# Summing a gate by matmuls on four column groups, in the result's row order, instead of a pass through DRAM

## The chip, the core and the metric

The kernel runs on one core of one Trainium2 chip. The metric is device microseconds of one execution, lower is better; the time of a kernel is the median of several runs. One further execution is taken by the hardware profiler, and all rows below are from it.

## The reference

Two blocks read the same `x` (`A_q`, 2048 rows of 640) and a gate per row mixes them. Block A is a short causal convolution of `k`, a product with `v`, a long convolution along the sequence (done by FFT) and a product with `x`. Block B is local attention with 32 heads of 20, a window of 8 keys at a distance of 2, between two projections.

```python
x = A_q
g = sigmoid((x * gate_w).sum(-1, keepdims=True))      # one number per row of x
a = A(x, A_k, A_v, A_shift_k, A_ssm_k, A_ssm_D)       # x * (longconv(kv) + kv * D)
b = B(x, B_wqkv, B_wo)                                # attention(x @ wqkv) @ wo
out = g * a + (1 - g) * b
```

## The kernel before

The kernel is one long stream of small units of work. Each unit (a generator step) asks a planner, `Plan`, for an engine, with a cost, with what it depends on and with a priority, and `Plan.run` decides at build time in which order the units stand on each engine and which of four PSUM slots (`ps0` to `ps3`, two banks each) a TensorE tile takes. On the chip each engine then works off its row in that order. A unit that must wait holds up all that stands behind it on its engine, and a tile whose slot is still to be copied out waits for that very slot, even if another is free: the slot is fixed by the plan.

The stages, in order of time:

- `transposes` (L423) bring x into `xT`, with the row order of the attention: even rows, then odd rows. `vproj` (L439, tiles `psv`) and `qkproj` (L480, tiles `pj`, one per feature tile `ft` and per q or k) project. Copies to SBUF go to ScalarE or VectorE, whichever the planner picks (helper lines L237 and L239). `conv` (L400, VectorE, tiles `pa`, `pb`) makes `kv`; its last step of each quarter (L418) needs the loads of v.
- Attention, in eight passes of four heads: `score_gen` (L552, tiles `sc`, ten groups a pass, an Exp on ScalarE at L572 each) and `pv_gen` (L579, tiles `O`, two a pass of 32 and 36 matmuls, divided into `oS` by VectorE at L610 and L612).
- `h_stream` and `u_stream`: two transforms in two steps, s1 (L631, 8 matmuls a unit) and s2 (L649, 32 matmuls a unit), with a copy of 1024 columns after each unit: to `Am` after s1, to `Hs` (h) or `Up` (u) after s2. The filter's transform h has 20 units of s1 and 20 of s2.
- `otrans` (L799), products of the two transforms (L758, L761), `inverse1` (L775), `inverse2` (L848), and `outproj` (L883), whose copies scale by `omg` = 1 - g (L892). The results stand by `[partition 32*gg + p, tile t]` for row 64*p + 16*gg + t.

The gate (L457) is a stream with priority 6 that waits for the transposes and for the first half of `vproj`. It makes 80 matmuls with 128 columns of `xT` as weights and one moving column (`wg`), which leave the sums in `xT`'s order in `gps`. ScalarE takes the Exp of the whole (L466), VectorE makes the sigmoid (L468, L469) in `g_chk`. Two DMAs on GpSimd's queue write it to DRAM (L471, L472), four read it back in the result's order into `g_nat` (L475), and VectorE makes `omg` (L477). `g_nat` is read again at L826, `omg` at L892.

Of the kernel before, what the change touches and what calls it, by code (L numbers as in the profile page):

```python
# [11 lines left out]
F32 = mybir.dt.float32  # L12
ACT = mybir.ActivationFunctionType
ALU = mybir.AluOpType
PSUM = bass.MemoryType.PSUM
DRAM = bass.MemoryType.DRAM

S = 2048
D = 640
# [3 lines left out]
NDT = 5  # L23
# [4 lines left out]
PRE = 7  # L28
HS = 1024 + PRE
# [73 lines left out]
def ccol(sb):  # L103
    return PRE + 128 * sb + (PRE if sb >= 8 else 0)
# [105 lines left out]
def kernel(  # L210
# [14 lines left out]
    nc = tc.nc  # L225
# [6 lines left out]
    def raw(ap, off, dims):  # L232
        return bass.AP(tensor=ap.tensor, offset=ap.offset + off, ap=dims)
# [7 lines left out]
    p0 = ctx.enter_context(tc.tile_pool(name="p0", bufs=1))  # L241
    psp = ctx.enter_context(tc.tile_pool(name="psp", bufs=1, space=PSUM, reuse_waits="tile"))
    plan = Plan(4)

    def psum(g, name, shape=(128, 2, 512), dt=F32, k=0):
        t_ = psp.tile(list(shape), dt, name=name, tag=f"ps{g.banks[k]}")
        return t_
# [8 lines left out]
    G = Gs[:].rearrange("p (a r b) -> p a r b", a=32, r=2)  # L256
# [2 lines left out]
    M = p0.tile([128, 2, 128], BF, name="M")  # L259
    g_nat = p0.tile([128, 16], F32, name="g_nat")  # L260
    omg = p0.tile([128, 16], F32, name="omg")
    g_chk = p0.tile([128, 16], F32, name="g_chk")
    dpool = ctx.enter_context(tc.tile_pool(name="scratch_dram", bufs=1, space=DRAM))
    g_scr = dpool.tile([S], F32, name="g_scr")
    valid = p0.tile([128, NB], BF, name="valid")
    wg = p0.tile([128, NDT], BF, name="wg")
    sH = p0.tile([128, 2 * KW], BF, name="sH")
# [19 lines left out]
    xT = pL.tile([128, NDT, XW], BF, name="xT")  # L287
# [10 lines left out]
    def ev(name):  # L298
        if name not in E:
            E[name] = Ev()  # L300
        return E[name]

    def mark(name, g):
        x = ev(name)
        x.t, x.eng = g.done.t, g.done.eng
# [130 lines left out]
    def xdeps(c):  # L436
        return [ev(f"xT{c}{d}") for d in (0, 4)]

    def vproj():  # L439
        for half in range(2):  # L440
            c0 = 320 * half
            for b0 in range(0, NB, 2):
                nb = min(2, NB - b0)
                g = yield Req("P", 5 * nb * 136.0, xdeps(min(3, (b0 + nb - 1) // 4)) + [ev("Wv")], take=1, pri=2 if half == 0 else 4)
                ps = psum(g, "psv")
                for bb in range(nb):
                    for dt in range(NDT):
                        nc.tensor.matmul(ps[:, bb, 0:320], lhsT=xT[:, dt, BP * (b0 + bb):BP * (b0 + bb) + 128], rhs=Wv[:, dt, c0:c0 + 320],  # L448
                                         start=(dt == 0), stop=(dt == NDT - 1))
                if b0 == NB - 1:  # L450
                    mark(f"vproj{half}", g)
                r = yield Req("AD", n=320 * nb, deps=[g.done], give=g.banks, pri=-2)
                copy(r.eng, VW[:, b0:b0 + nb, 16 * half:16 * half + 16, 0:DH].rearrange("p b h d -> p b h d"),
                     ps[:, 0:nb, 0:320].rearrange("p b (h d) -> p b h d", h=16))
            mark(f"VW{half}", r)

    def gate():  # L457
        g = yield Req("P", 2200.0, xdeps(3) + [ev("vproj0")], take=1)
        gps = psum(g, "gps", (128, 16))
        for sb in range(16):  # L460
            for dt in range(NDT):
                nc.tensor.matmul(gps[:, sb:sb + 1], lhsT=xT[:, dt, ccol(sb):ccol(sb) + 128], rhs=wg[:, dt:dt + 1],
                                 start=(dt == 0), stop=(dt == NDT - 1))
        mark("gatePE", g)
        r = yield Req("A", 250.0, [g.done], give=g.banks)
        nc.scalar.activation(g_chk[:], gps[:], ACT.Exp, scale=-1.0)  # L466
        r = yield Req("D", 500.0, [r.done])
        nc.vector.tensor_scalar(g_chk[:], g_chk[:], 1.0, None, ALU.add)  # L468
        nc.vector.reciprocal(g_chk[:], g_chk[:])  # L469
        r = yield Req("G", 1000.0, [r.done], move=2000.0)  # L470
        nc.gpsimd.dma_start(g_scr[:].rearrange("(h s p two) -> p two h s", p=128, two=2, h=1)[:, 0, 0, :], g_chk[:, 0:8])  # L471
        nc.gpsimd.dma_start(g_scr[:].rearrange("(h s p two) -> p two h s", p=128, two=2, h=1)[:, 1, 0, :], g_chk[:, 8:16])  # L472
        r = yield Req("G", 4000.0, [r.done], move=500.0)
        for q in range(4):
            nc.gpsimd.dma_start(g_nat[32 * q:32 * q + 32, :], raw(g_scr[:], 16 * q, [[64, 32], [1, 16]]))  # L475
        r = yield Req("D", 150.0, [r.done])
        nc.vector.tensor_scalar(omg[:], g_nat[:], -1.0, 1.0, ALU.mult, ALU.add)  # L477
        mark("gate", r)

# [444 lines left out]
    plan.add(conv(), 6)  # L924
    plan.add(transposes(), 1)
    plan.add(vproj(), 2)
    plan.add(gate(), 6)
    plan.add(qkproj(), 3)
    plan.add(h_diag(), 0)
    plan.add(h_stream(), 5)  # L930
# [42 lines left out]
```

## Time and profile before

| | |
|---|---|
| median of 3 runs (lowest to highest) | 305.73 us (304.98 to 306.28) |
| the profiled execution: its time | 305.71 us |
| the profiled execution: span of the profile | 303.9 us |
| TensorE matmul busy | 231.3 us (76%) |
| ScalarE busy | 180.9 us (60%) |
| VectorE busy | 173.8 us (57%) |
| GpSimd busy | 78.5 us (26%) |
| mean granted TensorE clock | 0.851 of full speed |

No engine is busy throughout, so busy shares alone say little: the stages have different limits. The profile's chain that ended last says for each stage what was waited for, and the rows of single engines say what a wait holds up. PE is TensorE, DVE VectorE, ACT ScalarE, POOL GpSimd. A row of a timeline is a run of like instructions; a bracket at its end is the idle time of the engine ahead of it and who ended that.

### The profile page before, as it was taken

Reading aid. Unit: us, or ns where it says so; the run is one execution under the profiler, and the core shown is the slowest. Engines: PE = TensorE matmul, PEld = TensorE weight load, DVE = VectorE, ACT = ScalarE, POOL = GpSimd, SP = SyncE. Lnnn points to the kernel's source line nnn. Section 1 sums busy time; section 2 is a strip of 40 time slices with the busy share of each in tenths; the row PEclk is TensorE's granted clock in tenths of the full one; section 3 lists DMA queues with packets and bytes.
Section 4 is the critical chain, followed back from the end, with each engine's and each line's share of the span. In section 5 each row is a group of like instructions: output and inputs, shape, how many; then the busy total and the mean of one; then the engine's idle time right before and its main releaser. Section 6 shows DMA issues by size and latency. Waiting matters only on the chain.

```text
span 303.9 us, 10648 instructions
## 1 busy us (share of the span) xinstructions
PE 231.3 (76%) x4825; PEld 169.7 (56%) x4825; DVE 173.8 (57%) x220; ACT 180.9 (60%) x218; POOL 78.5 (26%) x147
## 2 busy tenths in 40 slices
PE   2893999935999999877787359998949792985820
PEld 2662565512555576755575258787838672963610
DVE  0226191048789789655557068965857587626610
ACT  1342354832588897987867436786656534877520
POOL 9879455304216225310002200000000020003320
PEclk9999899985999999755559659999978897899795
DMA  6999998987294124798007800000360998004530
GB/s 223 355 172 150 143 173 152 165 139 99 67 167 92 23 72 89 128 183 340 6 2 94 188 3 4 4 4 2 80 202 9 226 218 177 2 5 121 146 88 0
DMA packets 57789, 34.33 MB, mean 113 GB/s; under 512 B 49848, under 2 KB 54460, under 8 KB 56720
## 3 DMA queue, kind: packets, MB, share of 16 engines
q1 hardware_dynamic: 52432, 23.50, 38.1%
q0 software_dynamic: 5312, 10.16, 16.3%
q8 instruction: 37, 0.61, 0.9%
q14 instruction: 8, 0.07, 0.1%
HBM read 20.33 MB, written 2.63 MB: 76 GB/s over the span
## 4 chain that ended last, share of the span: by engine, by line
PE 41%; SPq 19%; DVE 15%; ACT 7%; issue 7%; DMA 6%; POOL 1%; POOLq 0%; DVEq 0%; ACTq 0%
SPq L315 19%; PE i L775 8%; PE pj L501 7%; PE op L883 5%; PE sc L565 5%; PE O L598 4%; PE psv L448 4%; DVE Hs L758 3%; DVE Hw L761 3%; DVE Am L239 3%; PE s L649 3%; DMA g_scr<-g_chk 3%; PE s L631 3%; ACT ET L572 2%; DMA g_nat<-g_scr 2%
## 5 line engine op out<-in xcount | busy, mean ns | idle before, releaser
L572 ACT ACTIVATE ET<-sc 128x726 bf16<-128x726 f32 (+1 forms) x80 | 65.1, 861 | 19.9 <-PE sc L565 19.3
L501 PE MATMUL pj<-xT,Wqk 128*128 128x363 bf16 (+3 forms) x250 | 52.3, 360 | 4.7 <-DVE VW L239 4.6
L239 DVE CAST Am<-s 128x1024 bf16<-128x1024 f32 x25 | 30.0, 1222 | 18.7 <-PE s L631 18.7
L649 PE MATMUL s<-Am,Gs 64*128 64x64 bf16 x1280 | 29.5, 200 | 13.5 <-DVE Hs L239 7.3
L565 PE MATMUL sc<-qb,kb 31*128 31x121 bf16 x544 | 28.1, 249 | 14.6 <-DVE oS L612 8.7
L501 PEld LDWEIGHTS <-Wqk 128*128 128x128 bf16 x250 | 23.7, 101 | 25.6 <-issue 7.9
L649 PEld LDWEIGHTS <-Gs 64*128 64x128 bf16 x1280 | 26.1, 102 | 17.6 <-issue 16.1
L565 PEld LDWEIGHTS <-kb 31*128 31x128 bf16 x544 | 15.5, 105 | 28.9 <-issue 18.2
L448 PE MATMUL psv<-Wv,xT 128*128 128x320 bf16 x170 | 27.0, 310 | 1.3 <-DVE xT L239 1.2
L775 PE MATMUL i<-M,Hw 128*128 128x128 bf16 x160 | 25.4, 250 | 2.9 <-issue 2.9
L883 PE MATMUL op<-wo,Hb 128*32 128x512 bf16 (+1 forms) x640 | 26.0, 310 | 1.1 <-ACT yg L857 0.7
L237 ACT CAST Cm<-i 128x1024 bf16<-128x1024 f32 x20 | 19.9, 1024 | 10.8 <-PE i L775 10.8
L775 PEld LDWEIGHTS <-Hw 128*128 128x128 bf16 x160 | 22.1, 154 | 3.8 <-issue 3.8
L775 PE MATMUL i<-M,Hs 128*128 128x128 bf16 x128 | 21.8, 258 | 0.7 <-ACT Am L237 0.4
L237 ACT CAST Gs<-pj 128x968 bf16<-128x968 f32 (+5 forms) x15 | 11.7, 782 | 17.2 <-PE pj L501 17.0
L237 ACT CAST Up<-s 128x1024 bf16<-128x1024 f32 x14 | 13.7, 1021 | 13.8 <-DVE Hw L761 13.8
L883 PEld LDWEIGHTS <-Hb 128*32 128x32 bf16 x640 | 18.2, 137 | 6.2 <-issue 2.2
L448 PEld LDWEIGHTS <-xT 128*128 128x128 bf16 x170 | 16.3, 101 | 8.9 <-POOL ET L373 1.2
L814 POOL DMA_DIRECT2D qg<-in_A_q_dram x4 | 1.9, 490 | 73.2 <-PE s L631 73.2
L537 POOL DMA_DIRECT2D qb<-Gs x21 | 10.6, 505 | 33.1 <-PE sc L565 28.3
L598 PEld LDWEIGHTS <-ET 128*128 128x128 bf16 x544 | 16.2, 100 | 4.6 <-issue 3.5
L775 PEld LDWEIGHTS <-Hs 128*128 128x128 bf16 x128 | 18.0, 154 | 1.1 <-issue 0.4
(81 smaller groups left out, 391.8 us busy)
## 6 DMA issues: line engine op xcount, KB each, us to landing
Hw<-Hs SPq DMA_DIRECT2D x8, 512.0 KB, 5.8
xS<-in_A_q_dram SPq DMA_DIRECT2D x4, 640.0 KB, 8.3
Hb<-in_A_k_dram SPq DMA_DIRECT2D x8, 320.0 KB, 12.5
kv<-in_A_v_dram SPq DMA_DIRECT2D x16, 160.0 KB, 7.2
Hb<-in_A_ssm_k_dram SPq DMA_DIRECT2D x16, 160.0 KB, 3.9
qg<-in_A_q_dram POOLq DMA_DIRECT2D x4, 640.0 KB, 8.0
Gs<-cf_G SPq DMA_DIRECT2D x1, 2048.0 KB, 11.2
Wqk<-in_B_wqkv_dram SPq DMA_DIRECT2D x2, 800.0 KB, 15.0
```

Source lines behind the costliest of these rows:

```text
L237: nc.scalar.copy(dst, src)
L239: nc.vector.tensor_copy(dst, src)
L315: nc.sync.dma_start(dst, src)
L448: nc.tensor.matmul(ps[:, bb, 0:320], lhsT=xT[:, dt, BP * (b0 + bb):BP * (b0 + bb) + 128], rhs=Wv[:, dt, c0:c0 + 320], start=(dt == 0), sto ...
L501: nc.tensor.matmul(ps[:, i, 0:n], lhsT=Wqk[:, dt, w, 128 * ft:128 * ft + 128], rhs=rhs, start=(dt == 0), stop=(dt == NDT - 1))
L537: nc.gpsimd.dma_start(dst[r0:r0 + fb - fa, 0:wd], stg[fa - f0:fb - f0, 0:wd])
L565: nc.tensor.matmul(sc[:, hh, BP * bb:BP * bb + BP], lhsT=kb[r:r + DH + NF, 128 * b:128 * b + 128], rhs=qb[r:r + DH + NF, BP * b:BP * b + B ...
L572: nc.scalar.activation(ETs[e][:, :, 0:nw], sc[:, :, 0:nw], ACT.Exp, scale=SCALE)
L598: nc.tensor.matmul(O[:, o0:o0 + 21], lhsT=ET[:, hh, BP * bb:BP * bb + 128], rhs=VW[:, b, 4 * t + h4, :], start=True, stop=True, skip_group ...
L649: nc.tensor.matmul(o, lhsT=G[rows, j, rr, :], rhs=Am[rows, 2 * j + rr, :, :], start=(rr == 0), stop=(rr == 1), tile_position=(64 * c, 0), ...
L775: nc.tensor.matmul(o, lhsT=src[:, c, :, :, 8 * oc + il].rearrange("p q j -> p (q j)"), rhs=M[:, k, :], start=(k == 0), stop=(k == 1), skip ...
L883: nc.tensor.matmul(op[32 * gg:32 * gg + 32, n0:n1], lhsT=raw(a, HS * (t % 2) + t // 2 + 8 * gg, [a.ap[0], [32, 32]]), rhs=wo[:, ft, n0:n1] ...
```

## The change

The gate is summed in the result's row order. For each of 16 result tiles t and each of 5 feature tiles, four matmuls stand side by side on the four column groups of TensorE, each with 32 columns of `xT` at a step of 32 as weights (rows 64*p + 16*gg + t) and the one moving column of `wg`: 320 matmuls instead of 80. The Exp goes straight to `g_nat`, VectorE makes the sigmoid in place and `omg` right after. The two DMAs out, the four back, `g_chk` and the DRAM scratch are gone. The stream no longer waits for `vproj`, its priority goes from 6 to 3, and its cost to the planner from 2200 to 5000.

```diff
     def gate():
-        g = yield Req("P", 2200.0, xdeps(3) + [ev("vproj0")], take=1)
+        g = yield Req("P", 5000.0, xdeps(3), take=1)
         gps = psum(g, "gps", (128, 16))
-        for sb in range(16):
+        for t in range(16):
             for dt in range(NDT):
-                nc.tensor.matmul(gps[:, sb:sb + 1], lhsT=xT[:, dt, ccol(sb):ccol(sb) + 128], rhs=wg[:, dt:dt + 1],
-                                 start=(dt == 0), stop=(dt == NDT - 1))
+                a = xT[:, dt, 0:1]
+                for gg in range(4):
+                    nc.tensor.matmul(gps[32 * gg:32 * gg + 32, t:t + 1],
+                                     lhsT=raw(a, PRE + HS * (t % 2) + t // 2 + 8 * gg, [a.ap[0], [32, 32]]), rhs=wg[:, dt:dt + 1],
+                                     start=(dt == 0), stop=(dt == NDT - 1), tile_position=(0, 32 * gg), skip_group_check=True)
         mark("gatePE", g)
         r = yield Req("A", 250.0, [g.done], give=g.banks)
-        nc.scalar.activation(g_chk[:], gps[:], ACT.Exp, scale=-1.0)
-        r = yield Req("D", 500.0, [r.done])
-        nc.vector.tensor_scalar(g_chk[:], g_chk[:], 1.0, None, ALU.add)
-        nc.vector.reciprocal(g_chk[:], g_chk[:])
-        r = yield Req("G", 1000.0, [r.done], move=2000.0)
-        nc.gpsimd.dma_start(g_scr[:]..., g_chk[:, 0:8])
-        nc.gpsimd.dma_start(g_scr[:]..., g_chk[:, 8:16])
-        r = yield Req("G", 4000.0, [r.done], move=500.0)
-        for q in range(4):
-            nc.gpsimd.dma_start(g_nat[32 * q:32 * q + 32, :], raw(g_scr[:], 16 * q, [[64, 32], [1, 16]]))
-        r = yield Req("D", 150.0, [r.done])
+        nc.scalar.activation(g_nat[:], gps[:], ACT.Exp, scale=-1.0)
+        r = yield Req("D", 650.0, [r.done])
+        nc.vector.tensor_scalar(g_nat[:], g_nat[:], 1.0, None, ALU.add)
+        nc.vector.reciprocal(g_nat[:], g_nat[:])
         nc.vector.tensor_scalar(omg[:], g_nat[:], -1.0, 1.0, ALU.mult, ALU.add)
         mark("gate", r)
...
-    plan.add(gate(), 6)
+    plan.add(gate(), 3)
```

With it the planner's whole order changes. Line numbers fall by 3 behind the removed declarations and by 7 behind the gate. The rows below give order only.

VectorE, before: the row around the first `kv` product (L418). `pa` and `pb` are the convolution, `rd` and `oS` the division behind the first `O` tile.

```order
L415 TENSOR_TENSOR pa<-pa,pb 128x2560
L418 TENSOR_TENSOR kv<-pa,kv 128x16x2x80
L407 TENSOR_TENSOR pa<-Hb,wl 128x2560
L407 TENSOR_TENSOR pb<-Hb,wl 128x2560
L415 TENSOR_TENSOR pa<-pa,pb 128x2560
L610 RECIPROCAL rd_81<-O 121x32
L612 TENSOR_TENSOR oS<-O,rd_81 121x8x80
L239 CAST Gs<-pj 128x768
```

VectorE at the same place, now:

```order
L412 TENSOR_TENSOR pa<-pa,pb 128x2560
L468 TENSOR_SCALAR g_nat<-g_nat 128x16
L469 RECIPROCAL g_nat<-g_nat 128x16
L470 TENSOR_SCALAR omg<-g_nat 128x16
L415 TENSOR_TENSOR kv<-pa,kv 128x16x2x80
L404 TENSOR_TENSOR pa<-Hb,wl 128x2560
L239 CAST sH<-pj 128x968
L404 TENSOR_TENSOR pb<-Hb,wl 128x2560
L603 RECIPROCAL rd_77<-O 121x32
L605 TENSOR_TENSOR oS<-O,rd_77 121x8x80
```

All of the gate now stands ahead of the `kv` product, and behind it VectorE copies out a projection (`sH`, ft = 2 of q) after one step of the convolution instead of dividing an `O` tile after three.

TensorE, before: the ninth of the ten groups of scores of the first pass, whose tile takes the slot of the first `O` tile (freed by L612 on VectorE). A bracket names whose semaphore is waited for.

```order
L501 LDWEIGHTS Wqk
L501 MATMUL pj<-xT,Wqk 128x384
L565 LDWEIGHTS kb_87 [waits DVE_49]
L565 MATMUL sc<-qb_88,kb_87 128x121 [waits PE_49]
L565 LDWEIGHTS kb_87
```

TensorE, now: the sixth group of the first pass, whose tile takes the slot of the projection that VectorE copies to `sH`.

```order
L494 LDWEIGHTS Wqk
L494 MATMUL pj<-xT,Wqk 128x363
L558 LDWEIGHTS kb_83
L558 MATMUL sc<-qb_84,kb_83 128x121 [waits DVE_49]
L558 LDWEIGHTS kb_83
```

The first instruction of TensorE that waits for VectorE's work behind the `kv` product is now three groups of scores earlier; the first `O` tile, two runs of 5 and 10 projections and 10 matmuls of `psv`, which stood ahead of it, stand behind it. The 320 matmuls of the gate stand ahead of ft = 1, where the 80 stood behind the last `psv`.

VectorE, before: the row behind the last division of the attention.

```order
L612 TENSOR_TENSOR oS<-O,rd_82 121x4x80
L468 TENSOR_SCALAR g_chk<-g_chk 128x16
L469 RECIPROCAL g_chk<-g_chk 128x16
L239 CAST Hs<-s_2472 128x8x128
L239 CAST Hs<-s_2518 128x8x128
L239 CAST Am<-s_2597 128x4x64x4
L239 CAST Am<-s_2641 128x4x64x4
L239 CAST Am<-s_2689 128x4x64x4
L477 TENSOR_SCALAR omg<-g_nat 128x16
L239 CAST Hs<-s_2745 128x8x128
```

VectorE at the same place, now:

```order
L605 TENSOR_TENSOR oS<-O,rd_78 121x4x80
L239 CAST Am<-s_2876 128x4x64x4
L239 CAST Am<-s_2920 128x4x64x4
L239 CAST Am<-s_2965 128x4x64x4
L239 CAST Am<-s_3009 128x4x64x4
L239 CAST Am<-s_3053 128x4x64x4
L239 CAST Am<-s_3097 128x4x64x4
L239 CAST Hs<-s_3152 128x8x128
```

`omg` no longer stands between the copies of the filter's transform. Between the last `psv` and the last `O`, TensorE now has 9 units of s1 and 5 of s2 where it had 6 and 1, 228 matmuls of scores where it had 248, and no gate; from the last `O` to the first `tr` it has 11 and 10 units where it had 14 and 14.

## Rows read from the trace of the kernel before

**Rows 1.** The chain that ended last, in order of time: start us, us, what.
```profile
160.05 8.14 DMA g_scr<-g_chk
...
170.46 5.92 DMA g_nat<-g_scr
```

**Rows 2.** By stretch: window, length, busy us of PE, PEld, DVE, ACT, POOL, clock, DMA.
```profile
71.99:120.65 48.66, 48.32 (x664) 28.58 (x666) 40.78 (x47) 37.38 (x48) 19.50 (x39) 0.95 0.43 85
120.65:157.77 37.12, 29.32 (x684) 22.07 (x686) 21.11 (x30) 31.29 (x41) 4.52 (x9) 0.56 0.54 135
...
166.62:176.51 9.89, 2.82 (x83) 2.19 (x81) 0.01 (x2) 3.76 (x4) 2.03 (x4) 0.63 0.68 157
```

**Rows 3.** Timeline of VectorE, filter's transform: start us, us, instructions, idle before.
```profile
159.67 2.29 DVE L239 CAST Hs<-s 128x1024 bf16<-128x1024 f32 x2
162.57 2.36 DVE L239 CAST Am<-s 128x1024 bf16<-128x1024 f32 x2 [0.62 <-PE s L631]
165.40 1.22 DVE L239 CAST Am<-s 128x1024 bf16<-128x1024 f32 x1 [0.47 <-PE s L631]
176.51 0.18 DVE L477 TENSOR_SCALAR omg<-g_nat 128x16 f32<-128x16 f32 x1 [9.88 <-DMA g_nat<-g_scr]
```

**Rows 4.** Timeline of TensorE, same stretch and its two ends.
```profile
155.23 1.03 PE L649 MATMUL s<-Am,Gs 64*128 64x64 bf16 x32
156.08 0.62 PE L631 MATMUL s<-F1b,Hb 64*128 64x128 bf16 x8
...
177.86 1.04 PE L649 MATMUL s<-Am,Gs 64*128 64x64 bf16 x32 [7.33 <-DVE Hs L239]
...
184.07 2.56 PE L799 MATMUL tr<-ident,oS 121*128 121x121 bf16 x45 [0.18 <-ACT Hs L237]
```

**Rows 5.** Timeline of ScalarE, same stretch.
```profile
159.68 2.85 ACT L237 CAST Am<-s 128x1024 bf16<-128x1024 f32 x3
162.40 3.06 ACT L237 CAST Hs<-s 128x1024 bf16<-128x1024 f32 x3
```

**Rows 6.** Timeline of VectorE, around the first kv product.
```profile
64.86 1.49 DVE L418 TENSOR_TENSOR kv<-pa,kv 128x2560 bf16<-128x2560 bf16 x1 [17.79 <-DMA kv<-in_A_v_dram]
66.38 1.49 DVE L407 TENSOR_TENSOR pa<-Hb,wl 128x2560 bf16<-128x2560 bf16 x1
```

**Rows 7.** Timeline of TensorE, ahead of that product and after it.
```profile
41.24 12.00 PE L501 MATMUL pj<-xT,Wqk 128*128 128x484 bf16 x65
...
71.99 0.48 PE L565 MATMUL sc<-qb,kb 31*128 31x121 bf16 x6 [8.58 <-DVE oS L612]
```

**Rows 8.** Timeline of TensorE at full clock: what one run of each kind takes.
```profile
91.23 0.95 PE L501 MATMUL pj<-xT,Wqk 128*128 128x363 bf16 x5
...
95.30 1.26 PE L501 MATMUL pj<-xT,Wqk 128*128 128x512 bf16 x5
...
98.31 1.53 PE L448 MATMUL psv<-Wv,xT 128*128 128x320 bf16 x10
99.78 0.34 PE L565 MATMUL sc<-qb,kb 31*128 31x121 bf16 x6
100.05 0.97 PE L598 MATMUL O<-VW,ET 128*128 128x21 bf16 x32
...
101.22 0.99 PE L501 MATMUL pj<-xT,Wqk 128*128 128x384 bf16 x5
```

**Rows 9.** The chain: the gate's matmuls, and matmuls on column and row groups.
```profile
120.97 2.08 PE gps L462 x80
...
194.20 1.51 PE op L883 x38
...
268.25 0.95 PE i L848 x96
```

**Rows 10.** Tile view of the gate: durations ns min/median/max, first and last start.
```profile
L462 PE MATMUL gps<-wg,xT x80: 163/163/178, 120.9 to 122.9; 128*128 128x1 bf16 x80
```

**Rows 11.** Line view of outproj: 640 weight loads of 32 columns at a step.
```profile
L883 PEld LDWEIGHTS <-Hb x640: 131/134/162, 194.1 to 290.0; 128*32 128x32 bf16 x160
```

More of the change, by code (lines that the diff above doesn't have):

```diff
@@ L261 @@
     omg = p0.tile([128, 16], F32, name="omg")
-    g_chk = p0.tile([128, 16], F32, name="g_chk")
-    dpool = ctx.enter_context(tc.tile_pool(name="scratch_dram", bufs=1, space=DRAM))
-    g_scr = dpool.tile([S], F32, name="g_scr")
     valid = p0.tile([128, NB], BF, name="valid")
@@ L457, in gate @@
     def gate():
-        g = yield Req("P", 2200.0, xdeps(3) + [ev("vproj0")], take=1)
+        g = yield Req("P", 5000.0, xdeps(3), take=1)
         gps = psum(g, "gps", (128, 16))
-        for sb in range(16):
+        for t in range(16):
             for dt in range(NDT):
-                nc.tensor.matmul(gps[:, sb:sb + 1], lhsT=xT[:, dt, ccol(sb):ccol(sb) + 128], rhs=wg[:, dt:dt + 1],
-                                 start=(dt == 0), stop=(dt == NDT - 1))
+                a = xT[:, dt, 0:1]
[3 more added lines that the diff above has]
+                                     start=(dt == 0), stop=(dt == NDT - 1), tile_position=(0, 32 * gg), skip_group_check=True)
         mark("gatePE", g)
         r = yield Req("A", 250.0, [g.done], give=g.banks)
-        nc.scalar.activation(g_chk[:], gps[:], ACT.Exp, scale=-1.0)
-        r = yield Req("D", 500.0, [r.done])
-        nc.vector.tensor_scalar(g_chk[:], g_chk[:], 1.0, None, ALU.add)
-        nc.vector.reciprocal(g_chk[:], g_chk[:])
-        r = yield Req("G", 1000.0, [r.done], move=2000.0)
-        nc.gpsimd.dma_start(g_scr[:].rearrange("(h s p two) -> p two h s", p=128, two=2, h=1)[:, 0, 0, :], g_chk[:, 0:8])
-        nc.gpsimd.dma_start(g_scr[:].rearrange("(h s p two) -> p two h s", p=128, two=2, h=1)[:, 1, 0, :], g_chk[:, 8:16])
-        r = yield Req("G", 4000.0, [r.done], move=500.0)
-        for q in range(4):
-            nc.gpsimd.dma_start(g_nat[32 * q:32 * q + 32, :], raw(g_scr[:], 16 * q, [[64, 32], [1, 16]]))
-        r = yield Req("D", 150.0, [r.done])
+        nc.scalar.activation(g_nat[:], gps[:], ACT.Exp, scale=-1.0)
+        r = yield Req("D", 650.0, [r.done])
+        nc.vector.tensor_scalar(g_nat[:], g_nat[:], 1.0, None, ALU.add)
+        nc.vector.reciprocal(g_nat[:], g_nat[:])
         nc.vector.tensor_scalar(omg[:], g_nat[:], -1.0, 1.0, ALU.mult, ALU.add)
```

## The prediction

> **What bounds the kernel now.** I read the chain that ended last first, since the busy shares of the four engines (26% to 76%) name no single limit. It shows the gate's way through DRAM on the path: 8.14 us until the write has landed and 5.92 us until the read has [rows 1]. Then I took the rows of the engines at that place to see what this wait holds up. On VectorE the small instruction that makes `omg` waits 9.88 us for the read, and the copies of the filter's transform stand behind it [rows 3]. TensorE runs out of PSUM slots and sits idle for 7.33 us, until VectorE copies again [rows 4]; in that stretch of 9.89 us VectorE is busy for 0.01 us, TensorE for 2.82 and ScalarE for 3.76 [rows 2]. The reader is to see that the wait is not the gate's own: `omg` is first used much later, and what costs is the place in VectorE's row.
>
> The busy times by stretch tell the limits elsewhere. From 71.99 us to the last `psv` at 120.65 us TensorE is busy for 48.32 of 48.66 us, so it sets the pace there. From there to the last `O` at 157.77 us nobody is full: ScalarE 31.29 and TensorE 29.32 of 37.12 us, at a mean granted clock of 0.56, so mostly at the lower level of 1.2 GHz [rows 2]. Ahead of 71.99 us VectorE waits 17.79 us for the loads of v with the first `kv` product [rows 6], and TensorE waits 8.58 us for what stands behind that product [rows 7].
>
> **The change, part by part.** All sums are made against the profiled execution, 305.71 us, which is within 0.02 us of the median of the three runs (305.73).
>
> *The wait goes, and with it part of the transform's work.* `omg` now depends on ScalarE and VectorE alone and is made before the first `kv` product, so nothing of the round trip is left. Between the last `O` (157.77) and the first `tr` (184.07 [rows 4]) lie 26.3 us for 28 units, 14 of s1 and 14 of s2. Where the copies run without the wait, from 159.67 to 166.62 us, VectorE makes five [rows 3] and ScalarE six [rows 5]: 11 units in 6.95 us, 0.63 us a unit. The new order leaves 21 units in this stretch, since seven more stand ahead of the last `O`. So 21 x 0.63 = 13.2 us, and 1.3 us as before until the copies run densely: 14.5 us, which is 11.8 us less. Of these, 7 x 0.63 = 4.4 us are moved units and 7.4 us the wait itself. TensorE's idle time of 7.33 us and VectorE's of 9.88 us bound the latter from both sides; I stay near the lower end because ScalarE made four copies during the wait (3.76 us [rows 2]), which now take their own time. What is late next there is the rate of the copies.
>
> *The matmuls of the gate.* Before, 80 take 2.08 us, 26 ns each, behind the last `psv` [rows 9]. 320 on four column groups have no row here. From below: 96 small matmuls on row and column groups take 0.95 us, 10 ns each [rows 9], so 3.2 us. From above, if every load and its matmul went one after the other: 134 ns for the load of 32 columns at a step [rows 11] and 163 ns for a matmul of one column [rows 10], 297 ns, so 95 us. The nearest row is `outproj`, with the same weights, on the same four groups: 38 pairs in 1.51 us, 40 ns each, with 128 or 512 moving columns [rows 9]; 12.7 us at most, and with one moving column surely less. I take 26 ns, the row of the old gate: 8.3 us. The Trainium skill, page "TensorE: Matmul & The Clock Gate", section "The mechanism", speaks against the change: a load of weights overlaps a running matmul only if their row groups differ, and here all 320 use all rows; by it the sum would be that of the third rival below. The `outproj` rows disagree, since 134 ns of load alone, 38 times in a row, would be 5.1 us and not 1.51.
>
> *Where these matmuls lie, and the new stall.* They stand ahead of ft = 1, so at 41.24 us. What comes before TensorE's next wait for VectorE: the 65 projections of the row at 41.24 (12.0 us [rows 7]), five more of 363 columns (0.95) and five groups of scores (0.34 each, 1.7 [rows 8]), in all 14.6 us. So TensorE arrives at the sixth group of scores at 55.9 us plus the gate's time. The slot it needs is that of the projection which VectorE now copies after `kv` and one step of the convolution: the loads end the wait at 64.86 us as before, since no load is touched, then 1.49 to 66.38, 1.49 to 67.9 [rows 6], and 1.16 us for 968 columns (1.22 for 1024 [rows 3]): 69.1 us. TensorE thus waits 13.2 us less the gate's time, and the gate costs nothing up to 13.2 us; at 8.3 us that cover holds. If the cover were gone, its whole time would be on the path, as TensorE is the bound behind it. The two gate instructions on VectorE ahead of `kv` and `omg`, some 0.6 us, and ScalarE's Exp lie within VectorE's 17.79 us of waiting; the queue behind them is the `kv` product itself, which could not have started earlier.
>
> TensorE starts again at 69.1 instead of 71.99 us, 2.9 us earlier, but with more to do. Behind the wait now stand 5 projections of 363 columns (0.95), 10 of 512 (2 x 1.26), 10 of 384 (2 x 0.99), 10 of `psv` (1.53), one `O` of 32 (0.97) and six groups of scores (6 x 0.34), all of which stood ahead of it before: 10.0 us by durations, some 9.5 us when the overlap of one run with the next (0.05 to 0.07 us) is taken off [rows 8]. Since TensorE is full until the last `psv`, this ends at 120.65 - 2.9 + 9.5 = 127.25 us: **6.6 us later**. This is the price of the new order, and nothing in the diff tells it.
>
> *From the last `psv` to the last `O`.* TensorE's 29.32 us lose the gate (2.08) and three groups of scores (about 0.5 each at the lower clock, between 0.34 and twice that, 1.5) and gain three units of s1 (0.62) and four of s2 (1.03 [rows 4]), 6.0: 31.7 us. ScalarE's 31.29 us over 41 instructions lose three Exps, about 2.3, and have 29.0 us. So from below 31.7 us. From above, if TensorE's idle time of 7.8 us stays, 39.5. Part of that idle time came from the gate, whose tile held one of four slots through this whole stretch because its Exp stood behind the last of the attention on ScalarE; now it is free at the start. I take 34.0 us, a good third of the idle time: 3.1 us less than before.
>
> *Removed, at nothing.* Six DMAs leave GpSimd's queue; what stands behind them there, the load of q, waits for the u transform long after, so nothing moves.
>
> **The sum.** +6.6 - 3.1 - 11.8 = -8.3 us; all later work keeps its order. 305.71 - 8.3 = **297.4 us**.
>
> **The rivals.**
>
> 1. *TensorE's lateness doesn't carry* (290.8 us). If the copies on VectorE (40.78 of 48.66 us) and ScalarE (37.38) set the pace in part, the 9.5 us of extra work would hide and the 6.6 us fall away: 297.4 - 6.6. Against it stands 48.32 of 48.66 us. Chance 0.20.
> 2. *The stretch to the last `O` doesn't get shorter* (302.9 us). If TensorE stays at the lower clock, with seven more units and the idle time it had, the stretch takes 39.5 us instead of 34.0: 297.4 + 5.5. A wait of s2 for its table, whose load follows the last `kv` product and so is some 6 us later too, would end in the same place. For it: the mean clock of 0.56. Against it: the free slot. Chance 0.20.
> 3. *Slower: the gate's pairs run one after the other* (about 379 us). Beyond the cover of 13.2 us every nanosecond counts: with p per pair, 320 p - 13.2 us is added, and the change loses from 320 p = 13.2 + 8.3, p = 67 ns. At 297 ns it is 95.0 - 13.2 = 81.8 us: 297.4 + 81.8 = 379. Against it: 40 ns per pair in `outproj`, with far longer matmuls. Chance 0.04.
>
> That the change doesn't do what it says can't be here: `omg` has no DMA left to wait for.
>
> **How the numbers follow.** Forecast 0.56, rivals 0.20, 0.20 and 0.04. The range takes in both middle rivals with a little beyond, 290 to 303.5 us. A measurement of this kernel can tell some 0.5% from no change, so 304.2 us is the limit: forecast, the first rival and most of the second lie below it, 0.93 faster. The tail of the second beyond 304.2 gives 0.03 for no change, and the third 0.04 for slower.
>
> **What would show it.** Right: the 320 matmuls start at about 41 us and end in under 13; TensorE then sits idle to about 69 us, its wait ended by VectorE's copy to `sH`; the last `psv` ends near 127 us, the last `O` near 161, the first `tr` near 176, with no idle time of VectorE over 2 us in between. Wrong: a last `psv` near 121 us would say that TensorE was not the bound; a stretch to the last `O` of over 38 us would say that the moved units were not free; an idle VectorE before `tr` would say that another wait took the place of `omg`'s. My least certain term is the 3.1 us.

## The result, and the profile after

The changed kernel takes **292.59 us** (median, 290.68 to 296.11), the kernel before beside it 305.63 us (304.98 to 306.28): a ratio of 0.955, 95% interval 0.946 to 0.964. Two later measurements gave 0.968 (0.965 to 0.971) and 0.959 (0.953 to 0.966). So it is faster by 3 to 5%, 13.0 us in the first measurement where 8.3 were forecast, and inside the range of 290 to 303.5 us. The profiled execution took 296.11 us (span 294.3), the slowest of the four and 3.5 us above the median; the rows below are from it and are compared with the sum, not with the median.

Cut at the points that the prediction names, in us:

| stretch | before | forecast | after | two further profiles of after |
|---|---|---|---|---|
| to the end of the last `psv` | 120.65 | 127.25 | 124.38 | 127.32, 128.79 |
| to the end of the last `O` | 37.1 | 34.0 | 34.4 | 33.3, 33.5 |
| to the first `tr` | 26.3 | 14.5 | 17.6 | 15.1, 16.6 |
| from there to the end | 119.9 | 119.9 | 118.0 | 117.3, 118.2 |

The two further profiles are of `e0_after` (294.73 us, beside a median of 294.27) and `e10_after` (298.81 us, the slowest of its six).

The page first: granted clock by slice, the queue of code, and the chain's shares by engine.

```profile
PEclk9998695799999999985555789999968897898675
...
q8 instruction: 39, 0.64, 1.0%
...
PE 54%; issue 12%; DVE 10%; ACT 7%; POOL 7%; DMA 5%; DVEq 0%; ACTq 0%; POOLq 0%
```

SyncE's queue, 19% of the chain before, is gone from it: the chain no longer runs through the loads of v. TensorE has 54% instead of 41, and "issue" 12% instead of 7. The long fall of the clock (slices 19 to 22) was there before; that of the seventh and eighth slice is new, while one that the kernel before had in its tenth slice is gone.

The gate and what follows, TensorE's timeline (start, us, engine, line, operation, tiles, count, idle time before):

```profile
42.47 2.11 PE L461 MATMUL gps<-wg,xT 128*32 128x1 bf16 x136
45.02 1.99 PE L461 MATMUL gps<-wg,xT 128*32 128x1 bf16 x128 [0.44 <-issue]
49.57 0.97 PE L461 MATMUL gps<-wg,xT 128*32 128x1 bf16 x56 [2.56 <-issue]
50.48 9.00 PE L494 MATMUL pj<-xT,Wqk 128*128 128x484 bf16 x35
...
67.56 0.34 PE L558 MATMUL sc<-qb,kb 31*128 31x121 bf16 x6
...
69.01 2.04 PE L494 MATMUL pj<-xT,Wqk 128*128 128x363 bf16 x10
```

The gate takes 8.07 us, of which it runs 5.07: 15.5 ns a pair of load and matmul (128 in 1.99 us). At 67.56 stands the sixth group of scores, where TensorE waited 8.58 us before [rows 7] and was to wait until 69.1 now. It does not wait at all. VectorE's timeline shows why:

```profile
50.81 0.17 DVE L468 TENSOR_SCALAR g_nat<-g_nat 128x16 f32<-128x16 f32 x1 [3.29 <-ACT g_nat L466]
...
51.31 0.18 DVE L470 TENSOR_SCALAR omg<-g_nat 128x16 f32<-128x16 f32 x1
59.08 1.49 DVE L415 TENSOR_TENSOR kv<-pa,kv 128x2560 bf16<-128x2560 bf16 x1 [7.59 <-DMA kv<-in_A_v_dram]
...
65.31 1.17 DVE L239 CAST sH<-pj 128x968 bf16<-128x968 f32 x1 [3.21 <-PE pj L494]
```

`omg` is done at 51.49, and the loads of v end the wait for `kv` at 59.08 instead of 64.86 us [rows 6]; now VectorE waits for TensorE's projection (65.31), not the other way round. GpSimd's timeline has the difference that goes with it. Before:

```profile
47.73 1.02 POOL L537 DMA_DIRECT2D qb<-Gs  x2 [0.40 <-issue]
51.22 1.00 POOL L537 DMA_DIRECT2D kb<-sH  x2 [2.46 <-ACT sH L237]
52.21 1.97 POOL L537 DMA_DIRECT2D qb<-Gs  x4
54.37 0.50 POOL L537 DMA_DIRECT2D kb<-sH  x1 [0.19 <-issue]
55.24 0.50 POOL L537 DMA_DIRECT2D kb<-sH  x1 [0.38 <-DMA qb<-Gs]
56.63 0.99 POOL L537 DMA_DIRECT2D kb<-sH  x2 [0.89 <-DMA kb<-sH]
```

After:

```profile
47.78 1.01 POOL L530 DMA_DIRECT2D kb<-Gs  x2 [2.33 <-DMA kb<-Gs]
58.09 1.01 POOL L530 DMA_DIRECT2D qb<-Gs  x2 [9.29 <-ACT Gs L237]
63.59 1.00 POOL L530 DMA_DIRECT2D kb<-sH  x2 [4.49 <-ACT sH L237]
```

Before, twelve DMAs that gather fragments of q and k go out between 47.7 and 57.6 us, while v is loading. After, their projections start some 9 us later, and the first of the twelve goes out at 58.09. Whether that is the cause was tried below.

Busy time, granted clock and DMA share by stretch (answering to [rows 2]; columns: stretch, its length, then busy time of PE, PEld, DVE, ACT and POOL with counts, clock, DMA share, GB/s):

```profile
44.90:50.54 5.64, 2.97 (x185) 2.87 (x186) 2.59 (x2) 0.00 (x0) 1.52 (x3) 0.50 0.84 153
50.54:55.10 4.56, 4.56 (x14) 1.72 (x14) 0.60 (x3) 0.55 (x2) 0.00 (x0) 0.50 0.81 118
...
67.56:124.38 56.82, 55.62 (x768) 33.50 (x769) 47.04 (x52) 45.60 (x61) 20.48 (x41) 1.00 0.52 101
124.38:158.77 34.39, 28.74 (x735) 22.51 (x736) 23.24 (x32) 29.25 (x38) 4.54 (x9) 0.59 0.47 127
158.77:176.35 17.58, 10.82 (x409) 9.91 (x409) 10.97 (x12) 10.97 (x12) 0.00 (x0) 0.79 0.48 107
```

From 67.56 to the last `psv` TensorE is busy for 55.62 of 56.82 us: it sets the pace there, as before. The last row holds what is left of the stretch with the stall of 9.88 us [rows 3]. Its idle time on TensorE is of another kind now:

```profile
161.34 0.58 PE L642 MATMUL s<-Am,Gs 64*128 64x64 bf16 x28
165.14 0.29 PE L642 MATMUL s<-Am,Gs 64*128 64x64 bf16 x4 [3.22 <-issue]
...
172.71 0.23 PE L642 MATMUL s<-Am,Gs 64*128 64x64 bf16 x4 [0.40 <-DVE Hs L239]
175.06 0.93 PE L642 MATMUL s<-Am,Gs 64*128 64x64 bf16 x28 [2.12 <-issue]
```

The pauses of 3.22 and 2.12 us fall in the middle of 32 matmuls of one unit and wait for no other engine. VectorE, which was not to be idle for over 2 us here, waits for TensorE:

```profile
165.90 4.80 DVE L239 CAST Am<-s 128x1024 bf16<-128x1024 f32 x4 [2.91 <-PE s L624]
```

### The profile page after: what moved, and what is told of

Read it like the earlier page. It is cut to its first block, busy times and chain, and to the rows that moved or that the text cites. A ratio compares the mean times of both kernels' runs of the same rounds, so it can differ in the third digit from the quotient of the medians.

```text
span 294.3 us, 11121 instructions
## 1 busy us (share of the span) xinstructions
PE 236.7 (80%) x5065; PEld 174.2 (59%) x5065; DVE 179.3 (61%) x223; ACT 176.6 (60%) x215; POOL 74.3 (25%) x141
## 3 DMA queue, kind: packets, MB, share of 16 engines
q0 software_dynamic: 5120, 10.14, 16.6%
## 4 chain that ended last, share of the span: by engine, by line
PE 54%; issue 12%; DVE 10%; ACT 7%; POOL 7%; DMA 5%; DVEq 0%; ACTq 0%; POOLq 0%
PE pj L494 13%; PE i L768 8%; PE s L642 6%; PE op L876 6%; PE psv L445 5%; PE sc L558 5%; PE O L591 3%; DVE Hw L754 3%; DVE Hs L751 3%; ACT ET L565 3%; PE s L624 3%; DMA Hb<-in_A_k_dram 2%; DMA wg<-in_gate_w_dram 2%; DVE Am L239 2%; ACT Up L237 2%
## 5 line engine op out<-in xcount | busy, mean ns | idle before, releaser
L494 PE MATMUL pj<-xT,Wqk 128*128 128x363 bf16 (+3 forms) x250 | 54.1, 368 | 4.0 <-DVE VW L239 4.0
L239 DVE CAST Am<-s 128x1024 bf16<-128x1024 f32 x28 | 33.5, 1220 | 18.7 <-PE s L624 15.9
L642 PE MATMUL s<-Am,Gs 64*128 64x64 bf16 x1280 | 30.3, 204 | 11.3 <-issue 5.3
L558 PE MATMUL sc<-qb,kb 31*128 31x121 bf16 x544 | 26.4, 240 | 5.2 <-ACT ET L565 2.2
L445 PE MATMUL psv<-Wv,xT 128*128 128x320 bf16 x170 | 28.2, 319 | 1.5 <-DVE xT L239 1.2
L876 PE MATMUL op<-wo,Hb 128*32 128x128 bf16 (+1 forms) x640 | 26.3, 313 | 2.5 <-issue 1.7
L768 PE MATMUL i<-M,Hw 128*128 128x128 bf16 x160 | 26.2, 255 | 0.6 <-issue 0.6
L768 PE MATMUL i<-M,Hs 128*128 128x128 bf16 x128 | 22.8, 265 | 0.7 <-ACT Am L237 0.4
L237 ACT CAST Gs<-pj 128x968 bf16<-128x968 f32 (+5 forms) x16 | 12.2, 762 | 17.5 <-PE pj L494 17.4
L445 PEld LDWEIGHTS <-xT 128*128 128x128 bf16 x170 | 16.7, 103 | 9.8 <-POOL ET L370 1.2
L412 DVE TENSOR_TENSOR pa<-pa,pb 128x2560 bf16<-128x2560 bf16 x12 | 17.9, 1488 | 0.3
L404 DVE TENSOR_TENSOR pb<-Hb,wl 128x2560 bf16<-128x2560 bf16 x12 | 17.8, 1487 | 0.2
## 6 DMA issues: line engine op xcount, KB each, us to landing
Wqk<-in_B_wqkv_dram SPq DMA_DIRECT2D x2, 800.0 KB, 14.5
```

Of the source, the lines that this page charges most:

```text
L237: nc.scalar.copy(dst, src)
L239: nc.vector.tensor_copy(dst, src)
L404: nc.vector.tensor_tensor(dst[:], k_[:, 3 - j:19 - j, :], wl[:, j, :].unsqueeze(1).to_broadcast([128, 16, 160]), ALU.mult)
L412: nc.vector.tensor_tensor(pa[:], pa[:], pb[:], ALU.add)
L494: nc.tensor.matmul(ps[:, i, 0:n], lhsT=Wqk[:, dt, w, 128 * ft:128 * ft + 128], rhs=rhs, start=(dt == 0), stop=(dt == NDT - 1))
L558: nc.tensor.matmul(sc[:, hh, BP * bb:BP * bb + BP], lhsT=kb[r:r + DH + NF, 128 * b:128 * b + 128], rhs=qb[r:r + DH + NF, BP * b:BP * b + B ...
```

## The experiments

Each was timed with the kernel before on the same chip: 304.38 us beside `e0` to `e3`, 306.07 beside `e4` to `e8`, 303.73 beside `e9` to `e12`. Three questions: does the gate's time lie on TensorE's path, was the wait the whole cost of the old way, and why do the loads of v come earlier?

### The gate's length in its new place

`e0_after`: the changed kernel again.

> The changed kernel once more, as the yardstick for the runs beside it. Both theories: 290 to 296 us (its four runs lay between 290.7 and 296.1). Theory A (the gate lies on TensorE's path, since the loads of v land by about 59 us): the gate takes 8 us from about 42.5 us with two idle spells in it, VectorE's wait for kv ends near 59 us, TensorE does not idle at the sixth group of scores. Theory B (the prediction's: the gate is hidden under a wait for the loads): the early end of the loads was an accident of one execution; here kv ends near 64.9 us and TensorE idles at the sixth group of scores until about 69 us. If the idle spells of TensorE marked issue are what makes runs differ, the sum of those spells differs from the first profile (0.44, 2.56, 1.22, 3.22 and 2.12 us) by as much as the times do.

`e1_gate80`: 80 matmuls at the same place.

```diff
-                for gg in range(4):
-                    nc.tensor.matmul(gps[32 * gg:32 * gg + 32, t:t + 1], lhsT=raw(a, PRE + HS * (t % 2) + t // 2 + 8 * gg, [a.ap[0], [32, 32]]), ...
+                nc.tensor.matmul(gps[:, t:t + 1], lhsT=raw(a, PRE + HS * (t % 2) + t // 2, [a.ap[0], [8, 128]]), ...
```

> The gate in the new place with 80 matmuls instead of 320: weights of 128 columns at a step of 8, so that the sums stand in another order of partitions and the gate values meet other rows. Everything else, the order on all engines included, is as in the changed kernel. Theory A (the gate's time lies on TensorE's path): 80 at 26 ns take 2.1 us, some 6 us less than the 8.0 us of 320; the last psv, the last O and the end come up to 6 us earlier, 285 to 287 us, or less of a gain if the loads of v then land later again and TensorE waits for VectorE at the sixth group of scores. Theory B (hidden under the wait for the loads): no change, within 0.5% of the changed kernel. Theory C (the number of instructions that TensorE's queue must fetch matters, not their duration): the idle spells at 42 to 50 us vanish as well, and those behind 130 us keep their number but move.

`e2_gate640`: every tile's sums twice.

```diff
-        for t in range(16):
+        for t in [k // 2 for k in range(32)]:
```

> Each tile's gate sums are made twice, 640 matmuls, the result the same. Order on all engines as in the changed kernel. Theory A (on the path): the gate takes 16 to 21 us instead of 8.0, and the time grows by 8 to 13 us, to 299 to 304 us. Theory B (cover of 13.2 us less the gate's time, so 5.2 us left): 16 us would be 2.8 us over the cover, so 293 to 294 us. Theory C (the pauses of the instruction fetch are periodic): 1280 instructions are five pages of 256, so four or five idle spells of 0.4 to 2.6 us inside the gate, about 2 us of matmuls between each two.

Measured: `e0` 294.27 us (ratio 0.968), `e1` 292.36 us (0.952, 0.945 to 0.959), `e2` 305.68 us (0.994, 0.990 to 0.999). The gate in the profile of `e0`, one row for the whole tile and what ended TensorE's idle time in it:

```profile
L461 PE MATMUL gps<-wg,xT x320: 195/195/217, 41.3 to 54.0; 128*32 128x1 bf16 x160
...
  issue: 7.9, 2
```

In `e1`, and the sixth group of scores there, TensorE's timeline:

```profile
41.27 5.01 PE L460 MATMUL gps<-wg,xT 128*128 128x1 bf16 x80
...
65.14 0.34 PE L556 MATMUL sc<-qb,kb 31*128 31x121 bf16 x6 [2.45 <-DVE sH L239]
```

In `e2`:

```profile
42.62 4.11 PE L461 MATMUL gps<-wg,xT 128*32 128x1 bf16 x264
49.00 2.00 PE L461 MATMUL gps<-wg,xT 128*32 128x1 bf16 x128 [2.27 <-issue]
52.73 2.00 PE L461 MATMUL gps<-wg,xT 128*32 128x1 bf16 x128 [1.73 <-issue]
56.46 1.89 PE L461 MATMUL gps<-wg,xT 128*32 128x1 bf16 x120 [1.73 <-issue]
```

The same 320 matmuls took 8.07 us in one execution, 12.9 in `e0` and 10.7 in a third (`e10`): the matmuls run 5.1 us each time, the rest is pauses. `e1` takes 5.0 us and has no pause, but most of the 3.0 us gained are given back: TensorE waits 2.45 us for VectorE, whose `kv` starts at 60.99. Last `psv`: 123.52 with a gate of 5.0 us, 124.38 with 8.1, 128.79 and 127.32 with 10.7 and 12.9, 131.88 with 15.7. So up to some 8 us the length is nearly hidden, and beyond that 7.7 us more gate make it 7.5 us later. Theory A, that all of it lies on the path, is wrong for the changed kernel, and the prediction's cover of 13.2 us was too wide. The median of `e2` is 11.4 us above that of `e0`, more than the later `psv` explains; in its profile the part behind the first `tr` takes 120.7 us instead of 117.3, and TensorE's pauses marked issue there add up to 12.6 us instead of 7.2.

### The place, with the old gate

`e5_place` and, on the chip of `e10_after`, `e11_place`: 80 matmuls on contiguous weights and the pass through DRAM, at the new place. The instruction that makes `omg` stands further back too, so that the wait of `omg` is gone here as well.

```diff
-        g = yield Req("P", 2200.0, xdeps(3) + [ev("vproj0")], take=1)
+        g = yield Req("P", 5000.0, xdeps(3), take=1)
-        r = yield Req("G", 4000.0, [r.done], move=500.0)
+        r = yield Req("G", 4000.0, [r.done, ev("frag")], move=500.0)
-        r = yield Req("D", 150.0, [r.done])
+        r = yield Req("D", 150.0, [r.done, ev("oT")])
-    plan.add(gate(), 6)
+    plan.add(gate(), 3)
```

> The old gate, 80 matmuls on contiguous weights with the pass through DRAM, at the new place ahead of ft = 1; the reads from DRAM stand behind the last fragment on GpSimd's queue, omg behind oT on VectorE's. TensorE's order is that of the changed kernel but for the gate's own matmuls. Theory A (the place gives the gain, the 320 strided matmuls only cost): the gate takes 2.1 us (26 ns each), 6 to 10 us less than the 8.0 and 12.9 us measured for 320; half of that or more is given back as a wait for the loads of v at the sixth group of scores (2.45 us with a gate of 5.0 us); 289 to 291 us, 2 to 5 us below the changed kernel. Rival (the way through DRAM is what matters, so leaving it out gives the gain): 300 us or more. Rival (the two writes on GpSimd's queue hold up the fragments behind them): a later second set of scores, 295 us or more.

> The changed kernel again, beside the three below on one chip, so that they can be told apart. 0.955 to 0.968 of the kernel before, as in its two earlier measurements.

> The place alone (80 contiguous matmuls and the pass through DRAM at the new place) once more, on the same chip as the changed kernel. Theory A (the gate's 8 us fill a wait for the loads of v that TensorE otherwise has at that place, and keep the fragments from the loads' way): within 1.5% of the changed kernel on either side, although its gate takes 2.1 us instead of 8; TensorE idles 8 us at the sixth group of scores. Rival (the gate's time is on the path): 2% faster than the changed kernel.

Measured: `e5` 297.89 us (0.975, 0.965 to 0.985); `e10` 293.03 us (0.959, 0.953 to 0.966) and `e11` 294.78 us (0.971, 0.965 to 0.976). TensorE in `e5`:

```profile
41.41 2.14 PE L462 MATMUL gps<-wg,xT 128*128 128x1 bf16 x80
43.42 6.71 PE L501 MATMUL pj<-xT,Wqk 128*128 128x484 bf16 x35
...
66.45 0.49 PE L565 MATMUL sc<-qb,kb 31*128 31x121 bf16 x6 [8.17 <-DVE sH L239]
...
68.27 3.53 PE L501 MATMUL pj<-xT,Wqk 128*128 128x363 bf16 x10
```

The gate is 5.9 us shorter than in the changed kernel, and TensorE waits 8.17 us (4.79 in `e11`) for VectorE's copy. The last `psv` ends at 125.22 (122.78 in `e11`), as with the long gate. Both runs are slower than the changed kernel by some 1%, not faster (on one chip 0.971 beside 0.959, with intervals that touch): the 320 strided matmuls cost nothing in the total there. The place does not give the whole gain: `e4` below, beside `e5` on the same chip, has only the edit to `omg` and stands at 0.984, so the place adds about 1% to it, a step within the noise.

### The new gate in the old place

`e3_late`:

```diff
-        g = yield Req("P", 5000.0, xdeps(3), take=1)
+        g = yield Req("P", 2200.0, xdeps(3) + [ev("vproj0")], take=1)
-    plan.add(gate(), 3)
+    plan.add(gate(), 6)
```

> The new gate (320 matmuls, no DRAM pass) at the old place behind the last v projection, so that TensorE's order is that of the kernel before but for the gate's own matmuls, and no work is moved ahead of the last psv. Prediction's terms: the wait at omg falls away (7.4 us, at most 9.9 us), the gate costs 8.3 us instead of 2.1 us behind the last psv where TensorE is not full (0 to 6 us more). So 296 to 304 us; near 298 us if the gate hides there, near 304 us if it lies on the path. If the gain of the changed kernel came from the earlier place alone, this one stays at 305 us.

Measured: 302.33 us, ratio 0.994 (0.990 to 0.998). The two stretches behind the last `psv`:

```profile
120.34:164.55 44.21, 32.71 (x924) 25.11 (x926) 21.11 (x30) 31.38 (x41) 4.55 (x9) 0.54 0.48 114
164.55:183.41 18.86, 15.08 (x562) 13.17 (x561) 14.49 (x18) 14.49 (x17) 0.00 (x0) 0.81 0.51 115
```

From the last `O` to the first `tr` 18.86 us instead of 26.3: 7.4 us, the prediction's value for the wait. But the gate takes 8.9 us here instead of 2.1, and the stretch ahead grows from 37.1 to 44.2, by 7.1 us. Without the new place nearly all of the gain in this stretch is paid back.

### The waiting instruction alone

`e4_before_omg_off`: the kernel before, `omg` further back in VectorE's row. The planner then also puts two units of `outproj`, whose copies need `omg`, from a place some 10 us behind the first `tr` to the end; up to the first `tr` nothing else moves.

```diff
-        r = yield Req("D", 150.0, [r.done])
+        r = yield Req("D", 150.0, [r.done, ev("oT")])
```

> The kernel before, its pass through DRAM untouched; only the one VectorE instruction that makes omg is put behind the end of the transposes to oT, so that nothing of the transform stands behind its wait. Theory A (the cost was the place of the waiting instruction in VectorE's row): from the last O to the first tr some 18.9 us instead of 26.3, as in the run with the gate at the old place; the whole 7.4 us earlier, about 297 us beside 304.4 for the kernel before. Rival (the pass itself costs, by its six DMAs on GpSimd's queue or by what they load on the DMA engines): no gain, 304 us. Rival (the rate of the copies takes back what the wait gave): 2 to 4 us, 300 to 302 us.

Measured: 300.81 us, ratio 0.984 (0.976 to 0.993). From the last `O` to the first `tr` 21.1 us, 5.2 less than before, with the DRAM pass untouched. VectorE at the place where it waited 9.88 us:

```profile
160.91 2.36 DVE L239 CAST Hs<-s 128x1024 bf16<-128x1024 f32 x2 [0.27 <-PE s L649]
163.46 3.49 DVE L239 CAST Am<-s 128x1024 bf16<-128x1024 f32 x3 [0.20 <-PE s L631]
169.96 2.45 DVE L239 CAST Hs<-s 128x1024 bf16<-128x1024 f32 x2 [3.01 <-PE s L649]
```

The wait is gone. That only 5.2 and not 7.4 us come back lies at least in part in TensorE's pauses marked issue, 5.2 us in this stretch here against 3.0 in `e3`. The time lies where the rival of the copies' rate had it (300 to 302 us), but the row at 169.96 speaks against it: VectorE is idle for 3.01 us and waits for TensorE.

### Why the loads of v end earlier

`e7_before_hold`: the kernel before; one small copy on GpSimd reads the loaded half of v, so that twelve fragment DMAs behind it go out only when that half has landed.

```diff
+                if t == 1 and i == 6:
+                    nc.gpsimd.tensor_copy(hold[:], kv[:, 0:2, 0, 0])
                 nc.gpsimd.dma_start(dst[r0:r0 + fb - fa, 0:wd], stg[fa - f0:fb - f0, 0:wd])
```

> The kernel before with one small GpSimd copy from the loaded half of v ahead of the seventh fragment of the second set, so that GpSimd issues 12 of its fragment DMAs only when that half of v has landed. Nothing else moves on any engine. Theory A (the loads of v and the fragments share the DMA engines, and the later gate moved the fragments out of the way): VectorE's wait for kv ends at 59 to 61 us instead of 64.9, TensorE goes on 4 us earlier at the sixth group of scores, and the kernel ends up to 4 us earlier, 300 to 302 us. Rival (the loads have their own pace, and the early end in the changed kernel has another cause): kv at 64.9 us as before, the second set of scores later, 304 us or more.

Measured: 299.09 us, ratio 0.981 (0.971 to 0.991). GpSimd and, below, VectorE:

```profile
47.72 1.14 POOL L540 DMA_DIRECT2D kb<-Gs  x2 [2.98 <-DMA kb<-Gs]
59.04 0.19 POOL L539 COPY hold<-kv 128x2 bf16<-128x2 bf16 x1 [10.18 <-DMA kv<-in_A_v_dram]
59.57 1.02 POOL L540 DMA_DIRECT2D qb<-Gs  x2 [0.34 <-issue]
```

```profile
59.26 1.49 DVE L419 TENSOR_TENSOR kv<-pa,kv 128x2560 bf16<-128x2560 bf16 x1 [11.76 <-POOL hold L539]
```

`kv` starts at 59.26 instead of 64.86, as in the changed kernel, although no load was touched and no other instruction moved: the fragments hold up the loads of v. The last `psv` comes at 112.95 us, 7.7 us earlier, and this one line gains 7 us. TensorE goes on at 66.39 us, 5.6 us earlier than before, and the rest is the clock. Behind the wait of 8.58 us the granted clock is 0.50 until 76.95 us; behind the shorter wait it stays at 1.00, and the next five projections take 0.99 us instead of 1.78. Before and in `e7`:

```profile
72.41 1.78 PE L501 MATMUL pj<-xT,Wqk 128*128 128x384 bf16 x5
```

```profile
66.39 0.34 PE L568 MATMUL sc<-qb,kb 31*128 31x121 bf16 x6 [1.74 <-DVE oS L615]
66.66 0.99 PE L502 MATMUL pj<-xT,Wqk 128*128 128x384 bf16 x5
```

In the other profiles the hold brings `kv` to 58.7 to 60.3 us; without it, and with early fragments, it stands at 64.80 (`e3`), 65.44 (`e4`), 62.30 (`e5`) and 59.88 (`e11`). `e5` and `e11` are one program, so the size of this effect differs from execution to execution. In `e11` the loads end nearly as early as in the changed kernel although most fragments go out ahead of them, so that the later fragments are what let the loads through in the new order too is argued from `e7`, not shown.

### The pieces put together

`e8_place_hold` (`e5` with the hold), again as `e12_place_hold` on the chip of `e10`; `e9_hold_omg_off` is the kernel before with the edits of `e4` and `e7`.

> Both edits together: the old gate at the new place, and the fragments held until the first half of v has landed. Theory A: kv at 59 to 60 us, TensorE's wait at the sixth group of scores about 1.5 to 4 us shorter than with the place alone, 287 to 289 us. Rival (the held fragments come too late for the second set of scores): no gain or a loss against the place alone, 291 us or more.

> Place and hold together once more on the same chip, as the candidate for the fastest version: 0.96 of the kernel before, some 0.5 to 1% below the changed kernel if the shorter gate and the earlier loads both count, equal to it if the wait for the loads at 64 us is what sets both.

> The kernel before with the two small edits that each gained alone: omg behind oT on VectorE's row, and the fragments held on GpSimd until the first half of v has landed. Gate, its place and its pass through DRAM stay. Theory A (the two gains lie in different stretches and add up): 0.984 x 0.981 = 0.966 of the kernel before, 293 to 296 us, as fast as the changed kernel without one of its new instructions; the last psv near 113 us, 21 us from the last O to the first tr. Rival (the earlier start only moves the work against the next limit, and the copies of the transform take it back): 298 us or more.

Measured: `e8` 293.13 us (0.962, 0.954 to 0.969), `e12` 290.87 us (0.960, 0.955 to 0.964), `e9` 294.86 us (0.975, 0.970 to 0.980). Place and hold together are as fast as the changed kernel (0.959 on the same chip), not faster, and they still make the pass through DRAM: with its readers further back it costs nothing that can be seen here. The two small edits in the old order give 0.975, not 0.966: the first `tr` is at 171.37, 12.7 us earlier than before, but the part behind it takes 121.0 us instead of 119.9. In it, as in `e4`, two units of `outproj` stand later, and there is a long pause. TensorE in `e9`:

```profile
234.25 1.07 PE L652 MATMUL s<-Am,Gs 64*128 64x64 bf16 x61
242.27 0.95 PE L652 MATMUL s<-Am,Gs 64*128 64x64 bf16 x29 [6.95 <-issue]
```

At this place the kernel before waits 2.85 us, for ScalarE's `Up`. No version tried is clearly faster than the changed kernel; `e1` (0.952 beside 0.968) might be, but its rows would have to be put in order again.

## Why the prediction was right, point by point

The sum is right, and partly by luck. In the first profile the first `tr` comes at 176.35 us where 175.75 was forecast, because two errors cancel: the last `psv` is 2.9 us earlier than forecast, the wait's term 3.1 us smaller.

- **The wait of `omg` and the moved units (-11.8): right in kind, 0.6 to 3.1 us too large in the profiles.** 17.6, 15.1 and 16.6 us instead of 26.3, for 14.5 forecast. `e3` gives the wait alone, 7.4 us, the value taken; `e4` shows that it was the place in VectorE's row and not the pass through DRAM. What was missing are TensorE's own pauses: 3.22 and 2.12 us in this stretch of the first profile, without which it would be 12.2 us. They also brought the prediction's own sign of being wrong, an idle VectorE: 2.91, 2.81 and 2.57 us at a time in the three profiles. The 1.3 us until the copies run densely are 1.9 by the rows (157.77 to 159.67 [rows 3]).
- **320 matmuls at 26 ns, 8.3 us: right total in one profile of three, wrong make-up.** They run at 15.5 ns, 5.1 us in all, and pause for 3 to 8 us.
- **The gate hidden under TensorE's wait: wrong.** The failed step is "the loads end the wait at 64.86 us as before, since no load is touched". The first `kv` product starts at 59.08, 60.10 and 58.24 us in the three profiles. The gate moved the projections and with them the fragment DMAs, and `e7` shows in the old order that these hold the loads up by 5.6 us. So the cover is not 13.2 us: the gate and the wait left behind it add up to 7.5 us in `e1`, 6.9 in `e11` and 10.3 in `e5`. In the changed kernel it is used up, TensorE does not idle at the sixth group of scores in any of its profiles, and with longer pauses the gate shows (last `psv` at 127.32 and 128.79).
- **9.5 us more work behind the wait (+6.6 to the last `psv`): the work was about right, the start was off.** At full clock TensorE takes 56.82 us from the sixth group of scores to the last `psv` in the changed kernel and 46.55 us from its restart in `e7`, which has the old order: 10.3 us more. (The prediction counts six groups of scores among the moved work and the section on the change 15 projections; in TensorE's rows it is three groups and 25 projections.) But the sixth group came at 67.56, 70.50 and 70.56 us instead of 69.1, and with no wait ahead of it TensorE kept the full clock, while the kernel before, at 0.50 for 5 us behind its wait, takes 48.66 us. Result: +3.7 us in the first profile. The +6.7 us of `e0`, so near the forecast, are luck: TensorE did not wait there, its gate took 12.9 us. Rival 1 gave nearly the measured time (290.8), but by another mechanism, for TensorE stays full there.
- **The stretch to the last `O` (-3.1): right**, 34.4, 33.3 and 33.5 us for 34.0, so rival 2 did not come true. The new order takes seven more units into it, and it still gets shorter. That the freed slot does this was not tried.
- **All later work unchanged: off by 1.7 to 2.6 us**, in the same direction in all three profiles. TensorE's idle time behind the first `tr`, counted in gaps over 0.3 us, is 18.7 us before and 16.7 to 17.1 after. `e1` and `e2`, with the same order and no pass through DRAM either, take 120.5 and 120.7 us there, so it is not the missing pass; the cause stays open.
- **Slower, with pairs one after the other: no.** 15.5 ns a pair, 25 to 40 with the pauses, far from the 67 at which the change would have begun to lose. The rule of the Trainium skill that stood beside this rival (page "TensorE: Matmul & The Clock Gate", section "The mechanism") does not hold for these loads: 128 of them with their matmuls take 1.99 us, and at 131 ns, the shortest of these loads in the trace, they alone would be 17.

In the first profile these add to -9.6 us of span where -8.3 was forecast. The other 3.5 us by which the median lies below the profiled execution have no trace. The gate's pauses, which differ by 5 us between profiles, are a candidate; that stays open.

## What to carry to other kernels

Before pricing a moved instruction, follow what its engine then does later, down to the DMAs that hang on it, and ask which load shares the DMA engines with them: in `e7` that was worth 7.0 us, as much as the stall which the diff was about. A short instruction that waits for a long round trip costs by what stands behind it in its engine's row, and to put it further back is one line. And the cost of many tiny matmuls is not their duration times their count.

## What the runs showed of the hardware that was not expected

- **TensorE pauses on its own instruction stream.** In `e2` the gate stops after 264 pairs and then after every 128, that is every 256 instructions, for 1.7 to 2.3 us, while 128 pairs take 2.0 us. The code queue moved 39 packets and 0.64 MB in the changed kernel, some 16 KB each, so 256 instructions would be one packet at 64 bytes each. The traces tie the two together. Counted in loads and matmuls, the pauses lie behind 961, 1,217 and 1,473 in `e2`, and behind 961, 4,545 and 5,057 in the changed kernel (2.56, 3.22 and 2.12 us), always a multiple of 256 apart; in all six a code packet landed 1.4 to 1.7 us before TensorE went on. The 6.95 us in `e9` are of this kind: they lie behind 7,617, 26 times 256 further than 961, and end 1.3 us after a packet landed. Why that packet set off only 4.2 us into the pause stays open. All this fits the Trainium skill, page "Runtime: NRT & Kernel Launch", section "Instruction fetch mechanics", which has such blocks; its remark that crossing one is mostly hidden does not hold for pairs of 15.5 ns.
- **Weights at a step are slower to load than contiguous ones.** 80 matmuls take 2.14 us on contiguous columns (`e5`) and 5.01 us at a step of 8 (`e1`); 320 with a quarter of the columns run 5.07 us. At a step the time goes with the columns, 10,240 in both, not with the instructions; 32 contiguous columns at a time were not run. The rate was the same at either level of the clock: 136 pairs in 2.11 us ahead of 44.9 us, where the granted clock is 1.00, and 128 in 1.99 us behind it, where it is 0.50.
- **The gate leaves the clock low.** It stays at 0.50, the level of 1.2 GHz, until 55.10 us, and the 35 projections behind the gate take 9.00 us instead of 6.71 in `e5`. There the loss comes later, after its own wait: ten projections take 3.53 us instead of 2.04.
